# Where the load of the fifth expert buffer stands on SyncE: at the start of the program, or behind an operand move of pair 19

## The chip, the cores and the metric

The kernel runs on one core of one Trainium2 chip. The metric is the device time of one execution in microseconds (us); the time of a kernel is the median of its runs. TensorE (PE) multiplies matrices, VectorE (DVE), ScalarE (ACT) and GpSimd (POOL) work on tiles, and SyncE (SP) issues nearly all DMAs. Every engine works through its own instructions in a fixed order and waits for the others by semaphores.

## The reference

What is computed, cut to the core:

```python
# attention: q, k, v of 8 batches x 8 heads x 576 rows x 64
scores = (1 / sqrt(64)) * q @ k.T
scores = where(block(i) >= block(j), scores, -1e9)      # blocks of 64
attn = exp(scores - max) / (sum + 1e-9)
x = (attn @ v)  ->  4608 x 512
# soft mixture: 8 experts x 4 slots
logits = x @ phi                                       # 4608 x 32
d = softmax of logits over the rows;  c = over the slots
slot_out[e] = relu((d.T @ x)[e] @ w1[e]) @ w2[e]       # w1: 512 x 1024, w2: 1024 x 512
x = c @ slot_out
# bilinear layer
out = (((x @ W1) * (x @ W2)) @ W3) @ Wout
```

## The kernel before

**Attention** works on 32 pairs of heads, four for each batch. The loop `for n in range(N + 1)` in `Attn.run` walks through the string `ORDER` for each pair; it does the scores and exponentials of pair n (`Q..`, tile `sc`, lines 262 to 279), the row maxima of pair n + 2 (`M..`, tile `mx`, line 192), the products with `v` of pair n - 1, and the operands of pair n + 3 (`PH`, `PL`). To keep float32 accuracy each operand is a sum of two parts: `prep_hi` (ACT cast, line 151) makes the high part, `prep_lo` (GpSimd subtraction, line 159) the low part. They stand in the operand sets `set0` to `set3`, pair n in set n % 4. Of each pair, four DMAs from tile to tile (`move`, line 180, 288 KB each) put halves of these parts on other partitions: one by `PH`, three by `PL`. The last two of the three each overwrite what the one before read, so the three go one after another. `mx` of the pair needs all of them. The first three pairs are prepared by `prep_first` (lines 172 to 177), which has no moves; pair 3 is the first with moves.

The row maxima come in seven pieces, reduced by DVE (lines 196 and 202) into `bm`; `level2` (line 226, tile `l2`, with line 228 to `m`) takes the maximum of these with a mask, and `mra` (line 239, `mrow`) spreads it by TensorE; ACT's casts at lines 243 and 244 put it into the operand set. `acc` (line 295) is a sum of exponentials on GpSimd. In the trace the tiles `l2` and the operand sets have short names (`l`, `set`).

**Loads.** SyncE issues the query and key load of a pair (`raw`, 576 KB, line 137), `v` (line 144), the weights of the bilinear layer that are converted beside attention (`raw` from the weights, `raw64` in the order, line 654), two small `cs` moves for each batch (lines 428 and 429), and the expert weights, which `load_expert` reads (line 671). There are 16 of these, of 2048 KB each, for two matrices of eight experts, in a ring of five buffers; four buffers (`win0` to `win3`) lie where attention's tiles are and are loaded for the first time in its last four pairs. The fifth, `own`, lies by itself and is free from the start; its first load, i = 4, the first matrix of expert 2, is written in the program at `Q11` of n = 16, the middle of attention. Expert work reads it after attention, from 440 us on.

**Bilinear layer.** `wps` (line 730) forms the product of W3 and Wout beside the expert stage, from weights that DVE, ACT and GpSimd convert and split (lines 633 to 676). At the end `ab` (line 888) and its copy `abs` (ACT, line 891) and transposition `abT` (line 895) give two factors, copied into `own` (line 903, DVE and ACT). From these GpSimd forms `G16` (lines 927 to 929, tile `g_stage`) and DVE further products (lines 916 to 924). `Hp` (lines 938 and 944) multiplies with them; line 944 reads `G16`. Then a long row of matmuls (line 1042) makes the output.

**What sets the order.** The program isn't issued in the order in which it is written. A scheduler simulates a timeline and puts each instruction on its engine's queue when its inputs and its tile are free; the order on each engine is then fixed. `issue_after(x)` keeps what stands in it behind the instruction x. An instruction that is free early, such as the load of `own`, is put early.

Of the kernel before, what the change touches and what calls it, by code (L numbers as in the profile page):

```python
# [7 lines left out]
F32 = mybir.dt.float32  # L8
# [9 lines left out]
NB = 4  # L18
# [31 lines left out]
def warm(nc, keep, ps, n, w=128):  # L50

    for _ in range(n):
        nc.tensor.matmul(ps[:, 0:w], lhsT=keep["zeros"][:, 0:128], rhs=keep["zeros"][:, 0:w], start=True, stop=True)


class Attn:
# [120 lines left out]
        nc.gpsimd.tensor_tensor(R2[dn, 0:2 * S], raw[up], r1[up, 0:2 * S].bitcast(F32), op=ALU.subtract)  # L177

    def move(self, dst, src):
        self.nc.sync.dma_start(out=dst.bitcast(F32), in_=src.bitcast(F32))  # L180


    def max_tile(self, n, i):
# [349 lines left out]
    def run(self):  # L533
        nc, N = self.nc, self.n_pairs
        ML = self.ML
        LA = NB - 1
        self.load(0, 2)
        self.constants()
        for n in range(2, LA):
            self.load(n)  # L540
        warm(nc, self.keep, self.sc_p.tile([128, 1024], F32, tag="sc", name="warm"), WARM[0], 512)
        rows = []
        for n in range(ML):
            self.prep_first(n)
            if n == 0:
                self.constants2()
            for i in range(7):
                self.max_tile(n, i)
            self.level2(n)
            self.const_rows(n)  # L550
            row = self.mrow(n)
            rows.append(row)
            self.load_v(n)
        for m in range(ML, LA):
            if m < PF:
                with self.tc.issue_after(rows[0]):
                    self.prep_first(m)
            else:
                self.prep_hi(m)
                self.prep_lo(m)  # L560
        with self.tc.issue_after(row):
            for n in range(ML, NB):
                self.const_rows(n)
        self.load(LA)
        for n in range(N + 1):
            for t in (self.ORDER if n < N else self.LAST).split():
                k = int(t[1]) if t[1:].isdigit() else 0
                if t[0] == "M" and t != "MR":
                    self.max_tile(n + ML, k)
                elif t[0] == "Q":  # L570
                    self.qk_unit(n, int(t[1]), int(t[2]))
                    if t == "Q11" and self.after_scores:
                        if N - NB <= n < N:
                            self.after_scores(n - N + NB)
                        elif n == N // 2:
                            self.after_scores(NB)
                elif t[0] == "V":
                    self.pv(n - 1, k)
                elif t[0] == "A":
                    self.preadd(n, k)  # L580
                elif t == "PH":
                    self.prep_hi(n + LA)
                elif t == "PL":
                    self.prep_lo(n + LA)
                elif t == "L2":
                    self.level2(n + ML)
                elif t == "MR":
                    self.mrow(n + ML)
                elif t == "SU":
                    self.sums(n - 1)  # L590
                elif t == "LD":
                    self.load(n + LA + 1)
                    self.load_v(n + VL)
                elif t == "PT":
                    if n and n % NP_B == 0:
                        self.push_tail(n // NP_B - 1)
                elif t == "T":
                    self.step(1)
                elif t == "BG":
                    if self.background and n >= 1 and (n == 1 or n * 16 // BGP > (n - 1) * 16 // BGP):  # L600
                        with self.tc.issue_after(self.last_max[n + 1]) if n < BGF else nullcontext(), self.tc.issue_after(self.last_exp[n - 1]):
                            self.background.popleft()()
        while self.background:
            self.background.popleft()()
        self.step(100)
# [553 lines left out]
```

## Time and profile before

| | |
|---|---|
| median of 3 runs | 671.33 us (670.86 to 671.59) |
| profiled execution | 673.6 us |
| span of its instructions | 671.8 us |
| mean granted TensorE clock | 0.970 |
| busy: TensorE, DVE, POOL, ACT | 93%, 69%, 53%, 52% of the span |
| DMA | 141.45 MB, mean 211 GB/s |

The span runs from the first to the last instruction of the profiled execution; the time of that execution holds some 2 us around it. Roughly, attention fills the first 370 us and has its tail in the next 35, the expert stage with its weight loads lies beside that and reaches to about 515 us, and the bilinear layer the rest.

### The profile page before, as it was taken

How to read it: one execution, taken by the hardware profiler on the slowest of the kernel's cores; microseconds unless marked ns; L12 is line 12 of the kernel's file. 1: busy time of each engine (PE TensorE's matmuls, PEld its weight loads, DVE VectorE, ACT ScalarE, POOL GpSimd, SP SyncE). 2: the span in 40 equal slices, each digit the busy share in tenths (PEclk: the TensorE clock that was granted, in tenths of full speed). 3: DMA queues.
4: the chain of work that ended last, by engine and by line, in shares of the span. 5: the costliest groups of instructions: out<-in, count | busy, mean ns of one | idle time of the engine just before them, and what ended most of it. 6: DMA issues, size and time to landing. Idle time of an engine off the chain costs nothing. (4 is left out here: it accounts for less than half of the span.)

```text
span 671.8 us, 11777 instructions
## 1 busy us (share of the span) xinstructions
PE 622.7 (93%) x4423; PEld 454.3 (68%) x4423; DVE 460.2 (69%) x819; ACT 349.5 (52%) x645; POOL 354.0 (53%) x306
## 2 busy tenths in 40 slices
PE   4758989999999999999999998896999899999997
PEld 2646757777777777677777774533675487888886
DVE  8616766788859788577886466699863987555450
ACT  6653745656657575555656462244443425445541
POOL 8565785786768687766867471034323402122220
PEclk9987989999999999999999999797999999999999
DMA  9278687878788787778875859799991310755742
GB/s 315 71 189 222 163 217 185 200 194 221 211 213 219 199 223 173 212 198 217 219 180 129 286 190 349 292 381 401 398 385 59 112 54 25 252 184 183 255 155 94
DMA packets 53497, 141.45 MB, mean 211 GB/s; under 512 B 5928, under 2 KB 15656, under 8 KB 53416
## 3 DMA queue, kind: packets, MB, share of 16 engines
q1 hardware_dynamic: 53260, 140.63, 69.5%
q8 instruction: 35, 0.57, 0.4%
q14 instruction: 22, 0.18, 0.1%
q10 hardware_dynamic: 180, 0.07, 0.0%
HBM read 96.44 MB, written 10.32 MB: 159 GB/s over the span
## 5 line engine op out<-in xcount | busy, mean ns | idle before, releaser
L196 DVE TENSOR_REDUCE bm<-mx 128x8 f32<-128x512 f32 (+1 forms) x192 | 113.6, 618 | 44.8 <-PE mx L192 43.5
L262 PE MATMUL sc<-set 128*128 128x320 f32 (+4 forms) x704 | 132.6, 322 | 2.3 <-ACT set L244 1.3
L262 PEld LDWEIGHTS sc<-set 128*128 128x128 f32 x704 | 102.5, 197 | 12.6 <-issue 6.5
L192 PE MATMUL mx<-set 128*128 128x320 f32 (+4 forms) x384 | 87.9, 337 | 18.0 <-DMA set<-set 9.6
L295 POOL TENSOR_TENSOR acc<-PTa 128x640 f32<-128x640 f32 x31 | 49.8, 1606 | 83.1 <-PE sum L341 75.7
L192 PEld LDWEIGHTS mx<-set 128*128 128x128 f32 x384 | 67.2, 212 | 28.1 <-issue 9.7
L329 ACT COPY xT<-pv 128x320 f32<-128x320 f32 x64 | 25.6, 399 | 110.9 <-PE pv L327 97.9
L1042 PE MATMUL ops<-H,Ph 128*128 128x512 f32 x264 | 82.8, 395 | 0.0
L159 POOL TENSOR_TENSOR set<-raw,set 128x1152 fp32r<-128x1152 f32 x29 | 76.9, 2650 | 6.4 <-ACT set L151 6.4
L993 POOL TENSOR_TENSOR Pl<-rot,Ph 128x384 fp32r<-128x384 f32 x22 | 25.5, 1179 | 96.2 <-ACT Ph L991 96.2
L322 PE MATMUL pv<-PTa,v 128*64 128x320 f32 (+2 forms) x512 | 70.8, 376 | 0.0
L295 POOL TENSOR_TENSOR acc<-acc,PTb 128x640 f32<-128x640 f32 (+1 forms) x62 | 65.7, 1060 | 2.3
L271 ACT ACTIVATE PTa<-sc 128x960 f32<-128x960 f32 x64 | 59.3, 977 | 5.1 <-PE sc L262 5.1
L730 PE MATMUL wps<-wo,w 128*128 128x512 f32 x192 | 52.6, 417 | 6.8 <-ACT w L675 5.5
L1042 PEld LDWEIGHTS ops<-H,Ph 128*128 128x128 f32 x264 | 49.8, 189 | 11.9
L322 PEld LDWEIGHTS pv<-PTa,v 128*64 128x64 f32 x512 | 34.1, 138 | 28.8 <-issue 4.1
L1042 PE MATMUL ops<-H,Pl 128*128 128x512 f32 x132 | 52.2, 395 | 0.0
L730 PEld LDWEIGHTS wps<-wo,w 128*128 128x128 f32 x192 | 35.5, 194 | 22.7 <-ACT w L675 6.4
L1045 ACT COPY o<-ops 128x512 f32<-128x512 f32 x36 | 21.0, 587 | 56.6 <-PE ops L1044 56.4
L279 ACT ACTIVATE PTb<-sc 128x704 f32<-128x704 f32 x64 | 43.9, 693 | 8.7 <-PE sc L262 8.5
L322 PE MATMUL pv<-PTb,v 128*64 128x320 f32 (+1 forms) x256 | 43.5, 412 | 0.0
L676 POOL TENSOR_TENSOR w<-f,w 128x512 fp32r<-128x512 f32 x16 | 20.7, 1292 | 31.6 <-ACT w L675 31.1
(223 smaller groups left out, 1179.8 us busy)
## 6 DMA issues: line engine op xcount, KB each, us to landing
set<-set SPq DMA_DIRECT2D x116, 288.0 KB, 4.1
win<-in_moe_w SPq DMA_DIRECT2D x13, 2048.0 KB, 9.9
raw<-in_qk SPq DMA_DIRECT2D x31, 576.0 KB, 6.4
v<-in_v SPq DMA_DIRECT2D x32, 288.0 KB, 4.4
rot<-cs SPq DMA_DIRECT2D x44, 192.0 KB, 3.7
out<-o SPq DMA_DIRECT2D x11, 768.0 KB, 4.1
raw<-in_moe_w SPq DMA_DIRECT2D x16, 512.0 KB, 7.2
w3raw<-in_w3T SPq DMA_DIRECT2D x16, 512.0 KB, 11.0
```

Source lines behind the costliest of these rows:

```text
L159: nc.gpsimd.tensor_tensor(T1[:, 0:2 * S], self.raw.pop(n), flat(R1).bitcast(F32), op=ALU.subtract)
L192: nc.tensor.matmul(ps[:, o0:o0 + kn], lhsT=R1[:, h, q0:q0 + 128], rhs=T1[:, k0:k0 + kn], start=True, stop=True)
L196: self.last_max[n] = nc.vector.tensor_reduce(out, ps[:, 0:m].rearrange("p (n k) -> p n k", k=64), axis=AX.X, op=ALU.max).ins
L262: nc.tensor.matmul(ps[:, o0:o0 + qn * (qs.stop - qs.start)], lhsT=lt[:, k0:k0 + 128], rhs=rt[:, qs, q0:q0 + qn], start=st, stop=not st)
L271: nc.scalar.activation(out=PTa[:, h], in_=ps[:, 0:960], func=AF.Exp, scale=SCALE)
L279: self.last_exp[n] = nc.scalar.activation(out=PTb[:, S * h:S * h + w], in_=ps[:, 256:256 + w], func=AF.Exp, scale=SCALE).ins
L295: add = lambda o, a, b: eng.tensor_tensor(o, a, b, op=ALU.add)
L322: nc.tensor.matmul(ps[64 * h:64 * h + 64, q0 - lo:q1 - lo], lhsT=v[:, 128 * j + 64 * h:128 * j + 64 * h + 64], rhs=pt[:, h, o:o + q1 - q0] ...
L329: nc.scalar.copy(self.xTb[b % 2][:, p, lo:hi], ps[:, 0:hi - lo])
L730: nc.tensor.matmul(p, lhsT=a[:, o], rhs=b, start=c + i == 0, stop=c == 7 and i == 2)
L993: eng.tensor_tensor(Pl[:, k], p, Ph[:, k].bitcast(F32), op=ALU.subtract)
L1042: nc.tensor.matmul(ps, lhsT=a[:, k, r], rhs=b[:, k], start=n == 0, stop=False)
```

## The change

`move` keeps the last instruction that it issued. At `Q11` of n = 16 the load of `own` is put in `issue_after` with that instruction, the move that `PH` issued for pair 19. The load can't be put ahead of it any more.

```diff
     def move(self, dst, src):
-        self.nc.sync.dma_start(out=dst.bitcast(F32), in_=src.bitcast(F32))
+        self.last_move = self.nc.sync.dma_start(out=dst.bitcast(F32), in_=src.bitcast(F32)).ins
...
                         if N - NB <= n < N:
                             self.after_scores(n - N + NB)
                         elif n == N // 2:
-                            self.after_scores(NB)
+
+                            with self.tc.issue_after(self.last_move):
+                                self.after_scores(NB)
```

Lines behind the second place have numbers higher by two after the change. Since the load is no longer among SyncE's first DMAs, the scheduler orders other instructions anew, at three places.

**The start.** On DVE, in the first pairs, before (`set2_67` and `raw_142` are pair 2, `l2_199` and `m_201` the level-two maximum of pair 0, `bm1_120` and `l2_248` are pair 1):

```order
L228 TENSOR_REDUCE m_201<-l2_199 128x10
L196 TENSOR_REDUCE bm1_120<-mx_222 128x8
L196 TENSOR_REDUCE bm1_120<-mx_226 128x8
L196 TENSOR_REDUCE bm1_120<-mx_230 128x5
L196 TENSOR_REDUCE bm1_120<-mx_233 128x8
L196 TENSOR_REDUCE bm1_120<-mx_237 128x8
L196 TENSOR_REDUCE bm1_120<-mx_241 128x5
L202 TENSOR_REDUCE bm1_120<-mx_244 128x2x4
L172 CAST set2_67<-raw_142 64x1152
L174 CAST set2_67<-raw_142 64x1152
L226 TENSOR_TENSOR l2_248<-bm1_120,lmask_118 128x90
```

and on DVE at the same place after the change:

```order
L228 TENSOR_REDUCE m_201<-l2_199 128x10
L172 CAST set2_67<-raw_142 64x1152
L174 CAST set2_67<-raw_142 64x1152
L196 TENSOR_REDUCE bm1_120<-mx_222 128x8
L196 TENSOR_REDUCE bm1_120<-mx_226 128x8
L196 TENSOR_REDUCE bm1_120<-mx_230 128x5
L196 TENSOR_REDUCE bm1_120<-mx_233 128x8
L196 TENSOR_REDUCE bm1_120<-mx_237 128x8
L196 TENSOR_REDUCE bm1_120<-mx_241 128x5
L202 TENSOR_REDUCE bm1_120<-mx_244 128x2x4
L226 TENSOR_TENSOR l2_248<-bm1_120,lmask_118 128x90
```

The two casts of pair 2 moved from behind the seven reductions of pair 1 to ahead of them.

On GpSimd at the same place, before (`set3_68` and `raw_275` are pair 3, `raw_360` pair 4):

```order
L295 TENSOR_TENSOR acc_304<-PTa_277 128x2x320
L175 TENSOR_TENSOR set2_67<-raw_142,set2_67 64x1152
L295 TENSOR_TENSOR acc_304<-acc_304,PTa_277 128x2x192
L177 TENSOR_TENSOR set2_67<-raw_142,set2_67 64x1152
L295 TENSOR_TENSOR acc_304<-PTb_278,PTa_277 128x2x128
L159 TENSOR_TENSOR set3_68<-raw_275,set3_68 128x1152
```

and on GpSimd after:

```order
L175 TENSOR_TENSOR set2_67<-raw_142,set2_67 64x1152
L177 TENSOR_TENSOR set2_67<-raw_142,set2_67 64x1152
L295 TENSOR_TENSOR acc_304<-PTa_277 128x2x320
L159 TENSOR_TENSOR set3_68<-raw_275,set3_68 128x1152
L295 TENSOR_TENSOR acc_304<-PTb_278,PTa_277 128x2x128
L295 TENSOR_TENSOR acc_304<-acc_304,PTa_277 128x2x192
```

The operand work of pair 2 moved ahead of the first `acc`, and that of pair 3 behind the first `acc`.

**The middle.** On SyncE at pair 19 (`set3_68`; `set0_65` is pair 20, whose query and key load is `raw_2804`), before:

```order
L180 DMA set3_68<-set3_68 64x1152 x2
L137 DMA raw_2804<-in_qk 128x1152
L180 DMA set3_68<-set3_68 64x1152
L428 DMA cs_61<-cT_2460 4x32x128
L429 DMA cs_61<-cT_2460 32x64
L144 DMA v_2526<-in_v 128x576
L180 DMA set3_68<-set3_68 64x1152
L180 DMA set0_65<-set0_65 64x1152 x2
```

and on SyncE after:

```order
L180 DMA set3_68<-set3_68 64x1152
L673 DMA own_86<-in_moe_w1 128x4x1024
L180 DMA set3_68<-set3_68 64x1152
L137 DMA raw_2804<-in_qk 128x1152
L428 DMA cs_61<-cT_2460 4x32x128
L429 DMA cs_61<-cT_2460 32x64
L144 DMA v_2526<-in_v 128x576
L180 DMA set3_68<-set3_68 64x1152
L180 DMA set0_65<-set0_65 64x1152
L180 DMA set3_68<-set3_68 64x1152
```

The load stands between the first and the second of pair 19's four moves, and the last two of them moved behind other DMAs of the next batch.

**The end.** On TensorE at the hand-over to the bilinear layer, before (`w_5748` and `w_5786` are the last two converted pieces of W3):

```order
L895 MATMUL abT<-ident,abs 128x128 x4
L730 MATMUL wps<-wo,w_5748 128x512 x8
L730 MATMUL wps<-wo,w_5786 128x512 x12
L944 MATMUL Hp_5998<-W_5458,g_stage 32x512
L944 MATMUL Hp_5998<-W_5494,g_stage 32x512
L944 MATMUL Hp_5998<-W,g_stage 32x512 x5
L938 MATMUL Hp_5994<-g_stage_5874 128x512 x2
```

and on TensorE after:

```order
L897 MATMUL abT<-ident,abs 128x128 x4
L732 MATMUL wps<-wo,w_5748 128x512 x8
L946 MATMUL Hp_5998<-W_5458,g_stage 32x512
L946 MATMUL Hp_5998<-W_5494,g_stage 32x512
L946 MATMUL Hp_5998<-W,g_stage 32x512 x5
L732 MATMUL wps<-wo,w_5786 128x512 x2
L940 MATMUL Hp_5994<-g_stage_5874 128x512 x2
```

Seven matmuls of line 944 moved ahead of the last 12 of `wps`. On ACT at this place the copy `abs` moved two casts (line 991) forward; on DVE the last piece of the weight conversion moved backward.

## Rows read from the trace of the kernel before

**Rows 1.** Page, part 1: busy us (share of the span) and instructions.

```profile
PE 622.7 (93%) x4423; PEld 454.3 (68%) x4423; DVE 460.2 (69%) x819; ACT 349.5 (52%) x645; POOL 354.0 (53%) x306
```

**Rows 2.** Waits of TensorE: line, releaser, us in total, times, longest us.

```profile
PE mx L192 <- DMA set<-set: 9.6, 3, 5.7
PE mra L239 <- DVE m L228: 8.7, 4, 4.1
```

**Rows 3.** Timeline of SyncE's issues: start us, us of issuing, line, DMA.

```profile
7.11 0.43 SPq L671 DMA_DIRECT2D own<-in_moe_w x1
...
36.91 0.49 SPq L180 DMA_DIRECT2D set<-set  x1
```

**Rows 4.** DMA issues, 7.0 to 7.5 us: KB each, us to landing.

```profile
own<-in_moe_w SPq DMA_DIRECT2D x1, 2048.0 KB, 11.2
```

**Rows 5.** Timeline of DVE, start of attention: start us, us, line.

```profile
25.26 1.14 DVE L172 CAST set<-raw 64x1152 fp32r<-64x1152 f32 x1
...
27.11 2.65 DVE L226 TENSOR_TENSOR l<-bm,lmask 128x90 f32<-128x90 f32 x1
```

**Rows 6.** Timeline of GpSimd, start of attention; in brackets idle time, releaser.

```profile
24.23 1.55 POOL L295 TENSOR_TENSOR acc<-PTa 128x640 f32<-128x640 f32 x1 [7.36 <-DVE bm L196]
...
34.23 2.65 POOL L159 TENSOR_TENSOR set<-raw,set 128x1152 fp32r<-128x1152 f32 x1
...
39.12 2.62 POOL L159 TENSOR_TENSOR set<-raw,set 128x1152 fp32r<-128x1152 f32 x1
```

**Rows 7.** Timeline of TensorE, start of attention.

```profile
30.10 0.19 PE L239 MATMUL mra<-negI,m 128*2 128x64 f32 x1 [4.12 <-DVE m L228]
...
49.07 3.38 PE L192 MATMUL mx<-set 128*128 128x448 f32 x12 [5.66 <-DMA set<-set]
...
59.49 0.47 PE L192 MATMUL mx<-set 128*128 128x448 f32 x2 [2.21 <-ACT set L244]
59.80 0.94 PE L262 MATMUL sc<-set 128*128 128x256 f32 x6
```

**Rows 8.** Page, part 6: all moves and all `win` loads.

```profile
set<-set SPq DMA_DIRECT2D x116, 288.0 KB, 4.1
win<-in_moe_w SPq DMA_DIRECT2D x13, 2048.0 KB, 9.9
```

**Rows 9.** Timeline of ACT, start of attention.

```profile
35.85 1.81 ACT L271 ACTIVATE PTa<-sc 128x960 f32<-128x960 f32 x2
37.56 1.14 ACT L151 CAST set<-raw 128x1152 fp32r<-128x1152 f32 x1
```

**Rows 10.** DMA issues, 47.5 to 47.7 us.

```profile
set<-set SPq DMA_DIRECT2D x1, 288.0 KB, 7.8
```

**Rows 11.** Timeline of SyncE at pair 19.

```profile
219.03 1.93 SPq L180 DMA_DIRECT2D set<-set  x3
...
229.04 3.09 SPq L180 DMA_DIRECT2D set<-set  x3
```

**Rows 12.** DMA issues, 220.1 to 220.5 us.

```profile
set<-set SPq DMA_DIRECT2D x2, 288.0 KB, 5.0
```

**Rows 13.** Timeline of TensorE at pair 19.

```profile
234.73 0.81 PE L192 MATMUL mx<-set 128*128 128x448 f32 x3
```

**Rows 14.** Timeline of TensorE at pair 7.

```profile
93.95 0.47 PE L192 MATMUL mx<-set 128*128 128x448 f32 x2 [2.32 <-DMA set<-set]
```

**Rows 15.** Window: busy us of PE, PEld, DVE, ACT, POOL; clock; DMA share; GB/s.

```profile
90.00:100.00 10.00, 6.77 (x40) 5.45 (x37) 4.92 (x12) 4.66 (x7) 7.68 (x6) 0.83 0.91 231
```

**Rows 16.** Timeline of TensorE at the end of the expert stage.

```profile
526.51 0.66 PE L895 MATMUL abT<-ident,abs 128*128 128x128 f32 x4 [1.55 <-ACT abs L891]
526.93 5.24 PE L730 MATMUL wps<-wo,w 128*128 128x512 f32 x20
```

**Rows 17.** Timeline of DVE at the end of the expert stage.

```profile
528.14 0.89 DVE L903 COPY own<-abT 128x128 f32<-128x128 f32 x4
```

**Rows 18.** Timeline of GpSimd at the end of the expert stage.

```profile
531.38 0.79 POOL L929 TENSOR_TENSOR g_stage<-g_stage 128x128 f32<-128x128 f32 x1
```

## Prediction

> **What bounds the kernel now.** I read the views in this order: busy shares, the waits of TensorE, the timelines of the first 60 us, the granted clock by stage, and the landing times of DMAs. TensorE is busy 93% of the span [rows 1], so time comes only from stretches in which it stands still, or from a stand-still that is added. Its waits put the largest two at the start of attention: `mx`, the row-maximum matmul, waits 9.6 us in three places for the moves that fill an operand set, 5.7 us of it once, and `mra`, which spreads the maxima, waits 8.7 us for `m`, 4.1 us of it once [rows 2]. Both long ones lie before 50 us. After them the operands come just in time for a TensorE that hardly rests, so whatever the first pairs win or lose stays won or lost to the end.
>
> The load that is moved is SyncE's thirteenth DMA now, issued at 7.11 us and landing 11.2 us later [rows 3, 4], in a stretch in which TensorE waits for other things. That load itself is not what the start costs. What the order listing shows is that three places have another order after the change: the first five pairs, pair 19, and the hand-over to the bilinear layer. Each is a term of the sum.
>
> **The start (term A).** DVE and GpSimd now do the operand work of pair 2 (lines 172, 174 and 175) in front of the level-two maximum of pair 1 (line 226). The trace has line 172 at 25.26 us and line 226 at 27.11 us, and it takes 2.65 us there, beside a GpSimd operation of the other half [rows 5]. After the change the operand work stands behind `m` of pair 0, where DVE has idle time, and line 226 follows the seven reductions, which end at 25.2 us, where line 172 starts now. GpSimd's add `acc` runs from 24.23 to 25.78 us [rows 6]; letting line 226 wait for its end, and 0.6 us for it and line 228, gives `mra` at 26.4 instead of 30.10 us [rows 7]: 3.7 us. The 0.6 is what lies between the last two: 27.11 plus 2.65 is 29.76, `mra` 0.34 later, and 0.3 for a line 226 that nothing holds up. Without the wait for `acc` it would be 0.5 us earlier still, which is not counted. The row of line 226 [rows 5] is long where the two engines overlap; the Trainium skill, page "SBUF — State Buffer", section "Who interferes with whom", says that a DVE operation with two SBUF inputs and a GpSimd operation that reads SBUF exclude each other, the later one blocking fully. The 2.65 us agree with it; by it the 26.4 stands, without it 25.9.
>
> `mra` is not the end of it, for the next waits are `mx` of pairs 3 and 4. Pair 3's low part (line 159) is on GpSimd at 34.23 us for 2.65 us, behind the operand work of pair 2 and two `acc` adds [rows 6]. Afterwards it is the second operation behind the operand work, at 26.0 us, done at 28.7. Its first move leaves SyncE at 36.91 us now [rows 3], so at 28.7 then. Three moves follow one another, each waiting for the one before. With 4.1 us for each, the median of 116 moves [rows 8], the last lands at 41.0 us, against `mx` at 49.07 us [rows 7], 8.1 us sooner.
>
> Pair 4 then decides. Its ACT cast (line 151) is at 37.56 us, behind the two exponentials of 35.85 us [rows 9]; after the change it stands between those two. From `mra` to the first exponential are 5.75 us now (30.10 to 35.85), so that one begins at 26.4 plus 5.75 or 32.15 us, takes half of 1.81 us, and the cast ends 1.14 us later, at 34.2. Line 159 of that pair follows on GpSimd, which two adds may still hold for a moment, and ends at 36.9 to 37.5 us instead of 41.74 (39.12 plus 2.62) [rows 6]; I take 37.2. Now its chain of three moves lasts from there to `mx` at 59.49 us [rows 7], with 7.8 us for the second move [rows 10]. With 4.1 us for each the last lands at 49.5 us; with 7.8 for the second, as now, at 53.2. I take 51, nearer to the median because fewer loads are between them there, hence a gain of 8.5 us; nine matmuls that are now behind this `mx` are done ahead of it, 1.4 us more at 0.94 us for six [rows 7]. **A is minus 10.0** (9.9), and 7.7 and 12 are its ends: 53.2 us on one side, 49.5 and a lower clock less on the other. From pair 5 on every step comes with the same shift, TensorE's too, so the 10 us persist.
>
> **The middle (term B).** The load now stands on SyncE between the first move of pair 19 (`PH`) and its three other ones. In the trace the first of those three is the last of the three issued from 219.03 us on, and the last of them is the first of the three at 229.04 us [rows 11]. Queued behind the load are also the query and key load of pair 20, two `cs` moves and a `v` load. A load of 2048 KB lands in 9.9 us by the median of thirteen, a move at this place in 5.0 us [rows 8, 12]. If the move directly behind the load lands when it does, it is 4.9 us late, and the two moves that wait for it as well. The cover is small: the last move lands at 229.04 plus 4.1 or 233.1 us, and `mx` of pair 19 begins at 234.73 us [rows 13], so 1.6 us are covered and TensorE stands still for 3.3. A stand-still costs more than itself here: the one of 2.32 us at pair 7 stands in a stretch of 10 us with 0.83 of the full clock [rows 14, 15], 1.7 us in 10. I add that 1.7. **B is plus 5.0.** Its ends are 0, if the move doesn't wait for the load's packets, and 9, if the delay is the 11.2 us of this very load at the start [rows 4] and the loads queued between the moves add theirs: a stand-still of 5.6 us and two stretches of lower clock, 3.4 us.
>
> Here the trace decides little by itself, since it has no move directly behind a 2 MB load. By the Trainium skill, page "DMA: Bandwidth & Descriptors", section "Queues, rings and completion order", each DMA engine takes the descriptors of one issuing queue in ring order, which speaks against this change: the moves wait for the whole load. By that rule B is the 5.0; if moves could overtake, B would be 0.
>
> **The end (term C).** TensorE stands still for 1.55 us before `abT` at 526.51 us, then does 20 `wps` matmuls in 5.24 us, to 532.2 us [rows 16]. They hide the chain that makes `G16`: DVE's copies of `abT` at 528.14 us, ACT's copies, and three GpSimd operations, of which the last is at 531.38 us for 0.79 us [rows 17, 18]. `G16` is ready at 532.17, just in time for line 944. After the change the seven matmuls of line 944 stand ahead of the last 12 `wps`. The copy `abs` stands two casts earlier on ACT, so `abT` comes about 1.5 us sooner, but TensorE then has only eight `wps` (2.1 us) and reaches line 944 at about 527.6 us. DVE's copies are ahead of less work of the weight conversion, but still behind the products of line 990, and I get them at 527.1 to 528.1 us: `G16` at 531.2 to 532.2. So TensorE stands still for 4 us instead of 1.55, and 12 `wps` (3.1 us) are still to be done when it goes on: plus 2.2 to 3.1 us, of which I take 2.6. The stand-still of 4 us calls for a lower clock by the same row as above, 1.7 us [rows 14, 15]. **C is plus 4.3**, its ends 1.8 (no lower clock, earliest copies) and 5.5.
>
> The added line itself, and one DMA issue more or less at a place, cost nothing: SyncE is idle between moves. The rest of the differences in order, in the final stage, move one matmul and one output DMA and are counted as zero.
>
> **The sum.** Minus 10.0 plus 5.0 plus 4.3 is minus 0.7 us. The profiled execution took 673.6 us, its span 671.8, the median of the runs is 671.33 us; I take the difference against the median, for the profiled execution is 2.3 us above it. That gives 670.6 us. A measurement can tell about 0.2% from no change, 1.3 us, so faster means below 670.0 and slower above 672.7.
>
> **The rivals.**
> - *The queue in the middle is longer.* For it: behind the load are four other DMAs, and the second move of pair 19 queues behind pair 20's 576 KB. Against it: a median of 9.9 us already holds some queueing [rows 8]. B is then 9 and the time 674.6, slower. It decides when the stand-still at pair 19 exceeds 5.3 us: B is then above 7.0, and the sum above plus 1.3.
> - *The load is hidden.* If the moves behind it land in their usual 4 to 5 us, TensorE sees nothing at 234.73 us: 665.6. Against it: the raw loads behind the load at the start are not used until later, so nothing there shows an overtaking.
> - *The start gives back less.* If pair 4's second move takes 7.8 us as now, `mx` starts at 53.2 us, A is 7.7, and the time is 672.9.
> - *The end costs nothing.* If DVE's copies come 3 us earlier, because conversion work moved behind them, `G16` is ready when TensorE arrives: 666.3. Against it: the products of line 990 and the casts stand in front of them in either order.
> - *The change does not do what it says* is out: the order listing shows the load at its new place.
>
> **How the numbers follow.** The forecast of 670.6, own range 667.5 to 673.5, has a chance of 0.50; the longer queue 0.18; the hidden load 0.12; the weaker start 0.12; the free end 0.08. Each of A, B and C is larger than their sum, and both signs hold much. From the forecast 0.21 lies below 670.0, 0.18 within and 0.11 above; with the hidden load and the free end faster has 0.41, with about half of the weaker start same has 0.24, and slower 0.35. For 8 in 10 I take 665.4 to 675.0, which leaves out the outer parts of the hidden load and of the longer queue.
>
> **What would show it.** Right, if `mra` of pair 1 is at about 26.4 us and `mx` of pairs 3 and 4 at about 41 and 51; if the first move behind the load lands some 10 us after its issue and TensorE waits about 3.3 us for the moves at pair 19; if line 946 (944 before) waits about 4 us for GpSimd. Wrong, if `mx` of pair 4 still starts after 53 us, if pair 19 shows no wait or one above 5.3 us, if a later pair has a new wait, or if the waits come out as said and the clock does not fall after them (3.4 us less).

## The result and the profile after

The changed kernel takes 675.57 us, the kernel before 671.15 us by its 20 runs (671.33 by the three that the prediction had); the ratio is 1.0069, with a 95% interval of 1.0042 to 1.0095. It is slower by 0.7%, 4.4 us. One of the changed kernel's 20 runs, at 843.9 us with a mean granted clock of 0.659, is left out of the ratio. The forecast was 670.6, the range ended at 675.0. The profiled execution of the changed kernel took 674.65 us, its span is 672.8 us.

All three places of the prediction show in its profile. Waits of TensorE, with the columns of [rows 2]:

```profile
PE mx L192 <- DMA set<-set: 14.2, 5, 6.2
...
PE mra L239 <- DVE m L228: 5.4, 3, 3.3
PE Hp L946 <- POOL g_stage L931: 4.3, 1, 4.3
```

The wait for `m` has lost 3.3 us, the wait for moves has grown by 4.6 us and has a new longest one of 6.2, and `Hp` waits for `G16`, which it did not. The timeline of TensorE puts them in place; the first three lines answer to [rows 7], the fourth to [rows 13], the last three to [rows 16]:

```profile
26.27 0.19 PE L239 MATMUL mra<-negI,m 128*2 128x64 f32 x1 [1.25 <-DVE m L228]
...
39.67 1.71 PE L192 MATMUL mx<-set 128*128 128x448 f32 x6 [1.95 <-DMA set<-set]
...
51.48 0.69 PE L192 MATMUL mx<-set 128*128 128x448 f32 x3 [1.72 <-DMA set<-set]
...
233.10 1.19 PE L192 MATMUL mx<-set 128*128 128x448 f32 x3 [6.19 <-DMA set<-set]
...
521.04 0.66 PE L897 MATMUL abT<-ident,abs 128*128 128x128 f32 x4
521.45 2.10 PE L732 MATMUL wps<-wo,w 128*128 128x512 f32 x8
527.85 3.57 PE L946 MATMUL Hp<-W,g_stage 128*32 128x512 f32 x14 [4.30 <-POOL g_stage L931]
```

`mra` of pair 1 is 3.8 us earlier, `mx` of pair 3 9.4 us and of pair 4 8.0 us. Pair 19 then stands still for 6.2 us, and line 946 for 4.3 us. The landing of the move behind the load, as in [rows 12], and the granted clock behind both stand-stills (columns of [rows 15]):

```profile
set<-set SPq DMA_DIRECT2D x1, 288.0 KB, 13.5
```

```profile
225.00:240.00 15.00, 8.81 (x64) 7.31 (x61) 5.36 (x12) 6.26 (x10) 6.84 (x6) 0.77 0.89 234
```

```profile
527.00:537.00 10.00, 9.15 (x39) 5.22 (x40) 9.90 (x17) 2.56 (x5) 2.55 (x2) 0.83 0.08 22
```

To follow a shift through the program I took the start of `mra` of each pair, of the first `ab` matmul and of the last output matmul from TensorE's timeline. Five columns say where the time goes in the kernels below; the last column is the measured ratio to the kernel before with its interval. Each row is one profiled execution; before_again (the second row) and half_size were run only once, so they have no ratio.

| kernel | `mra` of pair 14 | pair 18 to 19 | pair 22 to 23 | pair 24 to `ab` | `ab` to last output | ratio |
|---|---|---|---|---|---|---|
| before | 187.8 | 12.2 | 15.5 | 212.2 | 147.6 | 1 |
| before, again | 186.5 | 12.2 | 12.2 | 210.2 | 148.4 | |
| changed | 178.3 | 20.6 | 12.2 | 210.9 | 152.7 | 1.0069 (1.0042 to 1.0095) |
| split | 181.5 | 12.2 | 17.7 | 212.3 | 152.7 | 1.0033 (1.0005 to 1.0062) |
| behind | 178.7 | 18.7 | 12.2 | 211.7 | 152.7 | 1.0026 (0.9993 to 1.0059) |
| half_size | 177.2 | 15.7 | 16.7 | 210.3 | 152.5 | |
| act_queue | 179.2 | 15.6 | 12.2 | 211.4 | 152.7 | 1.0027 (0.9996 to 1.0058) |
| end_fence | 177.7 | 20.0 | 12.2 | 213.8 | 156.6 | 1.0127 (1.0086 to 1.0167) |
| conv_first | 178.8 | 18.9 | 12.3 | 211.1 | 152.5 | 1.0061 (1.0032 to 1.0091) |
| conv_ahead | 179.4 | 21.3 | 12.2 | 214.0 | 148.8 | 1.0042 (1.0012 to 1.0072) |
| parts_conv | 179.5 | 13.5 | 15.8 | 211.8 | 152.6 | 1.0014 (0.9981 to 1.0047) |
| start_before | 187.4 | 20.6 | 12.2 | 213.0 | 148.2 | 1.0099 (1.0064 to 1.0134) |
| early | 182.9 | 12.2 | 12.2 | 212.9 | 147.6 | 0.9914 (0.9889 to 0.9940) |
| early_conv | 178.7 | 12.2 | 12.4 | 212.6 | 147.6 | 0.9924 (0.9900 to 0.9948) |

### The profile page after: what moved, and what is told of

Its sections match the earlier page's. It is cut to its first block, busy times and chain, and to the rows that moved or that the text cites. A ratio compares the mean times of both kernels' runs of the same rounds, so it can differ in the third digit from the quotient of the medians.

```text
span 672.8 us, 11771 instructions
## 1 busy us (share of the span) xinstructions
PE 618.5 (92%) x4423; PEld 450.0 (67%) x4423; DVE 460.3 (68%) x819; ACT 349.7 (52%) x645; POOL 355.5 (53%) x306
## 3 DMA queue, kind: packets, MB, share of 16 engines
q1 hardware_dynamic: 53260, 140.63, 69.7%
## 5 line engine op out<-in xcount | busy, mean ns | idle before, releaser
L262 PEld LDWEIGHTS sc<-set 128*128 128x128 f32 x704 | 103.5, 199 | 13.5 <-issue 4.8
L192 PE MATMUL mx<-set 128*128 128x320 f32 (+4 forms) x384 | 85.1, 326 | 20.7 <-DMA set<-set 14.2
L192 PEld LDWEIGHTS mx<-set 128*128 128x128 f32 x384 | 64.2, 201 | 30.9 <-issue 14.9
L159 POOL TENSOR_TENSOR set<-raw,set 128x1152 fp32r<-128x1152 f32 x29 | 77.0, 2654 | 11.3 <-ACT set L151 11.2
L995 POOL TENSOR_TENSOR Pl<-rot,Ph 128x384 fp32r<-128x384 f32 x22 | 27.6, 1273 | 96.1 <-ACT Ph L993 96.1
```

The source lines that it names most:

```text
L159: nc.gpsimd.tensor_tensor(T1[:, 0:2 * S], self.raw.pop(n), flat(R1).bitcast(F32), op=ALU.subtract)
L192: nc.tensor.matmul(ps[:, o0:o0 + kn], lhsT=R1[:, h, q0:q0 + 128], rhs=T1[:, k0:k0 + kn], start=True, stop=True)
L262: nc.tensor.matmul(ps[:, o0:o0 + qn * (qs.stop - qs.start)], lhsT=lt[:, k0:k0 + 128], rhs=rt[:, qs, q0:q0 + qn], start=st, stop=not st)
L995: eng.tensor_tensor(Pl[:, k], p, Ph[:, k].bitcast(F32), op=ALU.subtract)
```

## The experiments

My theory after this: the start gives some 8 us by the order of DVE and GpSimd, the load in SyncE's queue takes 8 us at pair 19, and the new order at the hand-over takes 4 to 5 us. The rivals stand in each expectation. Of each edit only the lines that matter are shown.

**before_again.** Expected: 

> The kernel before, unchanged, with a profile of another execution. If the wait of 1.67 us for pair 22's moves and the lower clock behind it belong to that one execution, this profile has no lower clock between 280 and 290 us and a span some 3 us shorter, or the same thing at another pair. If they belong to the order, they stand at the same place again, mx of that pair at 282.35 us.

The wait did not come back. (It is that of pair 23 in the count of this document; the expectation calls it 22.) In the kernel before the wait is this line of TensorE's timeline:

```profile
282.35 0.70 PE L192 MATMUL mx<-set 128*128 128x448 f32 x3 [1.67 <-DMA set<-set]
```

The same stretch of the two executions, columns of [rows 15], in the kernel before:

```profile
280.00:290.00 10.00, 8.33 (x56) 6.74 (x50) 5.01 (x11) 6.14 (x10) 7.82 (x6) 0.83 0.80 208
```

and in its second profile:

```profile
280.00:290.00 10.00, 10.00 (x80) 7.38 (x76) 8.10 (x15) 6.49 (x11) 8.79 (x7) 1.00 0.80 206
```

So 3.3 us of the first profile belong to one execution. A difference between two traces is read stage by stage, and 1 to 3 us at pairs 7, 15 and 23 are no evidence by themselves.

**split.** The load in four pieces, each behind the last move of a pair:

```diff
-                        elif n == N // 2:
-                            with self.tc.issue_after(self.last_move):
-                                self.after_scores(NB)
...
                 elif t == "PL":
                     self.prep_lo(n + LA)
+                    if 0 <= n - N // 2 < 4:
+                        with self.tc.issue_after(self.last_move):
+                            self.after_scores(NB, n - N // 2)
```

Expected: 

> The change, but the 2 MB load is cut into four of 512 KB, each behind the last move of one pair (19 to 22); every other engine has the order of the changed kernel. Theory (the moves of pair 19 wait for the whole load in SyncE's queue, 6.2 us and a lower clock, 8.4 in all): the wait of mx at pair 19 goes, no pair has more than 2 us in its place, and the time is 7 to 9 us below the changed kernel, 0.993 to 0.996 of the kernel before. Rival (the wait comes from where pair 19's moves stand among the other DMAs, or from 2 MB more of traffic in this stretch): waits of 2 us and more stay in this stretch, and the time is that of the changed kernel, 1.003 to 1.010.

Half of each. Pair 19 takes 12.2 us, as in the kernel before: the 8.4 us there are gone, with DVE, GpSimd, ACT and TensorE in the order of the changed kernel. But the time falls only to 1.0033, and a wait comes at pair 23, whose moves have the fourth piece ahead of them:

```profile
278.42 0.70 PE L192 MATMUL mx<-set 128*128 128x448 f32 x3 [3.90 <-DMA set<-set]
```

Pair 23 closes a batch like pair 19 and has the two `cs` moves in its queue. The pair takes 5.5 us more than 12.2; since one of the two executions of the kernel before lost 3.3 us there without any piece, how much of it the piece costs isn't shown.

**behind.** The whole load behind the last move of pair 19:

```diff
                 elif t == "PL":
                     self.prep_lo(n + LA)
+                    if n == N // 2:
+                        with self.tc.issue_after(self.last_move):
+                            self.after_scores(NB)
```

Expected: 

> The change, but the whole load stands behind the last move of pair 19, so that the first two moves of pair 20 stand directly behind it; the other engines have the order of the changed kernel. Theory (whichever move stands behind the load waits for all of it): the wait at pair 19 goes and one of 4 to 6 us for moves comes at pair 20; the time is within 2 us of the changed kernel, 1.004 to 1.010 of before. Rival (pair 19 is a special place, with two cs moves and a v load in its queue): no wait over 2 us at pair 20, time 0.993 to 0.997.

The loss stayed in size (6.5 us instead of 8.4), but the wait was another than I expected. Not pair 20's move decided, but a weight load for the conversion that stands behind the load: ACT waits for it (first line of the next two views), `lg` waits for ACT (second).

```profile
238.77 0.67 ACT L638 ACTIVATE m<-raw 128x512 bf16<-128x512 f32 x1 [8.64 <-DMA raw<-in_moe_w]
```

```profile
239.78 2.19 PE L383 MATMUL lg<-xT,phib 128*64 128x288 f32 x8 [4.92 <-ACT Lg L385]
```

Whatever stands behind the load waits, not the moves alone. Pair 20's moves were late too. Here the trace has the landing of the load, issued at 221.29 us, and of the second move behind it, issued at 222.91 us:

```profile
own<-in_moe_w SPq DMA_DIRECT2D x1, 2048.0 KB, 10.4
```

```profile
set<-set SPq DMA_DIRECT2D x1, 288.0 KB, 12.2
```

So the load landed at 231.7 us and this move 3.5 us later.

**half_size.** The first half of the load at the place of the change, the second behind the last move of pair 21:

```diff
                             with self.tc.issue_after(self.last_move):
-                                self.after_scores(NB)
+                                self.after_scores(NB, 0)
...
+                    if n == N // 2 + 2:
+                        with self.tc.issue_after(self.last_move):
+                            self.after_scores(NB, 1)
```

Expected: 

> The change, but only the first 1 MB of the load stands at its place behind the first move of pair 19; the second 1 MB stands behind the last move of pair 21. All engines but SyncE have the order of the changed kernel. Theory (the moves wait for the bytes ahead of them in the queue): the move behind the load lands 8.5 to 10 us after its issue instead of 13.5, and mx of pair 19 waits 1.5 to 3 us instead of 6.2. Rival (a fixed price of the place, whatever the size): the wait stays at 5 us or more.

In this one execution it came as the theory had it, but for 0.2 us: SyncE's timeline shows the move behind the load and, as the second line, the one that waits for its landing: 10.2 us, where 8.5 to 10 were expected, against 13.6 in the changed kernel (213.04 and 226.62).

```profile
208.75 1.19 SPq L180 DMA_DIRECT2D set<-set  x1
...
218.94 0.46 SPq L180 DMA_DIRECT2D set<-set  x1
```

The load itself, of 1 MB, was issued at 207.89 us and landed at 216.9 us, 2.0 us ahead of the move:

```profile
own<-in_moe_w SPq DMA_DIRECT2D x1, 1024.0 KB, 9.0
```

`mx` of pair 19 waits 1.9 us (the profile names ACT's line 243 as the releaser, but the last move landed at 226.14 us and `mx` starts at 226.23), and the pair takes 15.7 us, 3.5 more than before. The second half costs 4.6 us at pair 23.

**act_queue.** ACT issues the load, which is tied to ACT's cast of pair 19 in place of the move:

```diff
-        self.nc.sync.dma_start(out=v, in_=...)
+        (self.nc.scalar if i == NB else self.nc.sync).dma_start(out=v, in_=...)
```

Expected: 

> The change, but ACT issues the 2 MB load, behind its cast of pair 19, instead of SyncE; the bytes and the moment are about the same, and SyncE's moves have a queue without it. Theory (the price is the order within SyncE's queue): the moves of pair 19 land in 4 to 8 us, mx waits under 2.5 us there, and the time is 4 to 8 us below the changed kernel, 0.995 to 1.002 of before. Rival (2 MB more of traffic in this stretch slows every move, whatever the queue): the moves land 10 us and more after their issue and mx waits 4 us or more.

The wait is that of the theory, the landing that of the rival. The wait falls to 1.75 us and the pair to 15.6 us, 5.0 of the 8.4 us less. But the moves still land late, the two issued between 211.5 and 212.5 us (the last of pair 18, whose landing alone is recorded, and the first of pair 19) and pair 19's second at 214.0 us:

```profile
set<-set SPq DMA_DIRECT2D x2, 288.0 KB, 8.3
```

```profile
set<-set SPq DMA_DIRECT2D x1, 288.0 KB, 11.4
```

That is 8 to 11 us instead of 4 to 5: 2 MB more in this stretch delay a move of another queue as well. How much of the 5.0 us is the order within one queue isn't shown, since the moment wasn't the same: the load left at 208.24 us, 5.8 us before pair 19's second move, where in the changed kernel it left 0.8 us before it (212.22 and 213.04).

**end_fence.** Line 946 behind the last `wps`:

```diff
             def h_last(f):
                 g = f % 4
-                nc.tensor.matmul(Hp[4][32 * g:32 * g + 32], ...)
+                with tc.issue_after(self.last_wps):
+                    nc.tensor.matmul(Hp[4][32 * g:32 * g + 32], ...)
```

Expected: 

> The change, but line 946 may only stand behind the last wps matmul on TensorE. Start and middle are those of the changed kernel. Theory (4.3 us of wait for G16 and a lower clock behind it make the loss of 4.4 to 5 us at the end): no wait for G16, and the time is 4 to 5 us below the changed kernel, 0.999 to 1.002 of before. Rival (the conversion of the last piece of W3, which also moved, holds TensorE instead): TensorE waits for w at wps instead, over 2 us, and the time falls by less than 2 us.

The rival. The wait for `G16` is gone and TensorE waits for the last piece of W3 instead, over 6 us of the 11.6 in this line (the other 5.5 stand in the kernel before too); and the ratio is the highest of all:

```profile
PE wps L732 <- ACT w L677: 11.6, 2, 6.2
```

**conv_first.** The copies of `abT` behind the last conversion:

```diff
+                        with tc.issue_after(self.last_f if m == 0 else self.last_hi):
-                        eng(dst[:, 4 * h:4 * h + 4, ...], v[:, :, m, h])
+                            eng(dst[:, 4 * h:4 * h + 4, ...], v[:, :, m, h])
```

Expected: 

> The change, but DVE's and ACT's copies of abT may only stand behind the conversion of the last piece of W3 (as in the kernel before); TensorE's order listing then has abT, 20 wps and line 946 again. Start and middle are those of the changed kernel. Theory (the loss of 4 to 5 us at the end comes from the conversion having moved behind the copies, which leaves TensorE only 8 wps to do while G16 is made): no wait over 1 us for G16, the wait of 1.5 us for abs may come back, and from the first ab matmul to the last output matmul it takes what it takes in the kernel before, 147.6 us, instead of 152.7; time 0.999 to 1.002 of before. Rival (the wait for G16 is due to GpSimd and stays whatever TensorE has to do): 151 to 153 us there, 1.005 to 1.009.

Neither came as written, though the stretch and the time lie in the rival's range. There is no wait for `G16`, but the same time, 4.3 us in two waits, is spent in waiting for the converted weights (3.6 us for ACT, 0.7 for GpSimd), and the stretch takes 152.5 us, nearly what it took without this remedy:

```profile
524.89 0.73 PE L732 MATMUL wps<-wo,w 128*128 128x512 f32 x2 [3.63 <-ACT w L677]
```

So putting back TensorE's order and the place of the copies doesn't take the loss away.

**conv_ahead.** The last two conversions in front of `soT`:

```diff
-                nc.vector.tensor_copy(dst..., p[:, 0:128])
+                with tc.issue_after(self.u_ops[-1]) if name == "soT" else nullcontext():
+                    nc.vector.tensor_copy(dst..., p[:, 0:128])
...
-            nc.scalar.copy(sos, so)
+            with tc.issue_after(self.m_ops[-2]):
+                nc.scalar.copy(sos, so)
```

Expected: 

> The change, but the copy soT may only stand behind the first step of the last conversion on DVE, and ACT's copy sos only behind the last but one squaring of a conversion, as both do in the kernel before. Start and middle are those of the changed kernel; TensorE has 20 wps ahead of line 946 again. Theory (in the changed kernel two conversion steps stand behind soT on DVE, which waits 11.7 us for sumT, so that the last two pieces of W3 come late; that, not TensorE's order, is the loss at the end): neither a wait of over 1 us for G16 nor one for w at wps; from the first ab matmul to the last output matmul 147.5 to 149 us instead of 152.7; time 0.998 to 1.002 of before. Rival (the loss is there as soon as the end starts with a lower clock or other traffic, whatever DVE's order): 151 us and more, 1.004 to 1.009.

In the changed kernel DVE stands idle in front of `soT` while a conversion is queued behind it:

```profile
515.80 0.29 DVE L784 COPY soT<-sumT 128x128 f32<-128x128 f32 x1 [11.71 <-PE sumT L782]
```

That gap alone is not the difference: in the kernel before DVE stands idle there too, 7.8 us for ACT and 1.7 in front of `soT`. What differs is what comes behind: the last step of the last conversion (line 641, 643 after) starts 6.6 us after the first `ab` in the kernel before (7.4 in its second profile), 12.1 us in the changed kernel and 6.8 us in conv_ahead.

With the conversions ahead, from the first `ab` on 148.8 us are needed, as the theory says, 3.9 less, and neither `G16` nor `w` is waited for over 1 us there. But `sos` and `soT` now come later, and 2.3 us of new waits stand ahead of `ab`:

```profile
518.05 1.08 PE L782 MATMUL sumT<-sel,sos 128*128 128x32 f32 x8 [0.92 <-ACT sos L881]
...
520.81 1.07 PE L892 MATMUL ab<-wA,soT 128*32 128x512 f32 x2 [1.37 <-DVE soT L785]
```

From pair 24 to the last output it is 362.8 us against 363.6 in the changed kernel and 358.6 to 359.8 in the kernel before. By the time the loss shrinks from 1.0069 to 1.0042, with intervals that overlap. The place of the conversion on DVE carries the wait for `G16`; that this alone is the loss isn't shown.

**parts_conv.** Pieces behind the moves of pairs 19, 20, 21 and 23, together with conv_first:

```diff
+                    if n - N // 2 in (0, 1, 2, 4):
+                        with self.tc.issue_after(self.last_move):
+                            self.after_scores(NB, min(n - N // 2, 3))
```

Expected: 

> Two remedies together: the load in four pieces of 512 KB, each behind the last move of a pair (19, 20, 21 and 23, so that none stands ahead of the moves of pair 23), and the copies of abT behind the last conversion as in conv_first. Theory (the start gives 8 to 10 us, the middle and the end took them): 661 to 665 us, 0.985 to 0.992 of before, with no wait over 2 us for moves between 200 and 300 us. Rival (the gain of the start is given back at the later pairs 7, 15 and 23 anyway, since their moves come just in time): 0.994 to 1.000.

The expectation failed: 1.0014, no change that can be told. No wait for moves above 2.0 us is left between 200 and 300 us, but three waits of 1.1 to 2.0 us remain: of `lg` for ACT at pair 19, of `mx` at pair 22, for which the profile names no releaser, and of `mx` for moves at pair 23. These pairs take 1.4, 3.5 and 3.6 us longer, 8.5 together (pair 23 without a piece ahead of its moves, as in one execution of the kernel before), and the end is as slow as in conv_first.

**early.** The load at the start, behind the query and key loads of pairs 2 and 3:

```diff
         self.load(LA)
+        with self.tc.issue_after(self.last_load):
+            self.after_scores(NB)
```

Expected: 

> The load of own stands at the start again, but behind the query and key loads of pairs 2 and 3 instead of ahead of them; DVE and GpSimd have the order of the changed kernel in the first pairs, and TensorE has line 946 behind all wps, as before. Theory (the 10 us at the start are the order of DVE and GpSimd, not the 2 MB, which land while the queue is idle): mra of pair 1 at 26 to 27 us, mx of pair 4 at 50 to 53 us, no wait at pair 19 beyond 2 us; time 0.984 to 0.992 of before. Rival (the 2 MB in the first 20 us are themselves the loss): mx of pair 4 at 55 us or later and the time 0.996 to 1.002.

665.98 us, 0.9914 of the kernel before: the lowest ratio of all. The load is issued at 17.62 us (SyncE's timeline), and `mra` of pair 1 comes as in the changed kernel (TensorE's):

```profile
17.62 0.43 SPq L671 DMA_DIRECT2D own<-in_moe_w  x1
24.79 0.56 SPq L180 DMA_DIRECT2D set<-set  x1
```

```profile
26.49 0.19 PE L239 MATMUL mra<-negI,m 128*2 128x64 f32 x1 [1.91 <-DVE m L228]
...
53.54 1.89 PE L192 MATMUL mx<-set 128*128 128x448 f32 x6 [5.05 <-DMA set<-set]
```

The next move comes 7 us after it, so the load has that stretch nearly to itself (343 GB/s from 18 to 25 us). `mx` of pair 4 is at 53.5 us, half a microsecond beyond what the theory allowed and 2.1 us later than in the changed kernel, but pair 19 takes 12.2 us and the end 147.6. The start isn't quite that of the changed kernel: ACT's cast of pair 4 stands behind both exponentials, so that GpSimd's line 159 of that pair starts at 35.77 us instead of 34.09. `mra` of pair 4 is at 64.4 us (63.2 in early_conv), where the changed start gives 59.7 to 62.7, and the gain in time, 5.8 us, is less than the 8 of the start.

**early_conv.** early and conv_ahead together. Expected: 

> As early, with the two conversion orders of conv_ahead besides. Theory (each of the two remedies takes away its own loss, and the end of early has nothing left to gain): within 0.3% of early. Rival (the end of early still loses by the conversion behind soT): 2 to 5 us below early.

0.9924, within the interval of early: at this end the second remedy has nothing to give.

**start_before.** The start of the kernel before, the rest changed:

```diff
-                with self.tc.issue_after(rows[0]):
+                with self.tc.issue_after(rows[0]), self.tc.issue_after(self.last_max[1]):
                     self.prep_first(m)
```

Expected: 

> The change, but the operand work of pair 2 may only stand behind pair 1's row maxima on DVE, as in the kernel before. The load keeps its place at pair 19; TensorE's order at the end comes out as before (20 wps ahead of line 946). Theory (the 8 to 10 us of the start come from the place of pair 2's operand work; the load at pair 19 costs 8 us): mra of pair 1 at 29 us or later instead of 26.3, mx of pair 4 between 52 and 59 us instead of 51, the wait at pair 19 again 4 to 6 us, so some 0 to 8 us from the start, 8 of loss in the middle and none at the end: 1.000 to 1.014 of before. Rival (the start is faster because the 2 MB are out of its way, whatever DVE's order): mra of pair 1 at 26 to 27 us, mx of pair 4 at 51 us, and the time 0.996 to 1.001.

The theory. With no 2 MB at the start, but with the two casts of pair 2 in front of line 226 again, `mra` of pair 1 and `mx` of pair 4 are back near where they were in [rows 7], and pair 19 waits as in the changed kernel:

```profile
29.81 0.21 PE L239 MATMUL mra<-negI,m 128*2 128x64 f32 x1 [3.31 <-DVE m L228]
...
58.10 1.19 PE L192 MATMUL mx<-set 128*128 128x448 f32 x3 [4.20 <-DMA set<-set]
...
242.07 1.19 PE L192 MATMUL mx<-set 128*128 128x448 f32 x3 [5.93 <-DMA set<-set]
```

It takes 1.0099. `mra` of pair 4 is at 69.7 us, 70.0 in the mean of the two profiles of before: with the old order the start is as slow without the 2 MB as with them. So the gain of the start is order, not bytes; early agrees, with the 2 MB at the start and `mra` of pair 1 at 26.5 us.

## Why the prediction was wrong

**Right: which three places, and the sign of each.** No fourth place shows that differs beyond what the two profiles of the kernel before differ by.

**Right in kind, 1.8 us too large: the start.** Predicted were `mra` at 26.4, `mx` of pair 3 at 41 and of pair 4 at 51 us; the trace has 26.27, 39.67 and 51.48. `mra` of pair 14 is at 178.9 us in the mean of the nine kernels with the changed start and the load not at the start, 187.1 in the mean of the two profiles of before: 8.2 us, where term A said 10.0. At pair 4 the same means are 60.6 and 70.0, 9.4 us. Most of what A took too much is in its last step, that everything after pair 4 keeps its distance: pair 7, whose moves have little slack, gives 1.1 us back (17.5 us from `mra` of pair 6 to that of pair 7, 16.4 in the kernel before).

**Wrong: the size of the middle.** This is the step that failed. The kind was right (the move behind the load, 1.6 us of cover, a lower clock after it), and so was the pair. Term B let the move behind the load land with the load, 9.9 us after its issue by [rows 8]; it landed after 13.5 us (12.5 to 13.5 in the five kernels with the load at this place), the wait was 6.2 us instead of 3.3, and the stretch lost 8.4 us instead of 5.0.

Two things in that step were wrong. The 9.9 us are not the median of thirteen loads: the trace of the kernel before has the landing of only three `win` loads, after 7.6, 9.9 and 20.2 us. And the moves behind a load landed after it, not with it: the second of them 3.5 us after it in behind, the first 2.0 us in half_size (by the issue of the move that waits for it). The landing of the load itself isn't recorded in the changed kernel, so how the 3.6 us divide between the two stays open.

The traffic has a part as well, though no run shows its size alone. Nine of the thirteen `win` loads run when SyncE has nothing but weights to load, at 381 to 401 GB/s (page, part 2, 437 to 504 us). Around pair 19 the same engines carried 261 GB/s from 212 to 226 us (the view of DMA traffic, changed kernel; kernel before, 7.5 to 18.3 us, behind it):

```profile
DMA packets 1005, 3.65 MB, mean 261 GB/s; under 512 B 93, under 2 KB 156, under 8 KB 1002
```

```profile
DMA packets 1169, 3.92 MB, mean 363 GB/s; under 512 B 93, under 2 KB 93, under 8 KB 1169
```

By these rates 2 MB take 8.0 us around pair 19 and 5.8 us at the start, an estimate. The DMA share of 0.74 to 0.96 from 210 to 240 us in the profile before said that there was little room; I read the landing time and not the share.

**The end: right in size, its cause only in part.** The wait for `G16` is 4.3 us where 4 was said, a lower clock follows (0.83), and from `ab` to the last output it takes 152.7 instead of 147.6 to 148.4 us, 4.3 to 5.1, where term C said 4.3. What I called the cause, TensorE's order, is only where it shows: with that order undone (end_fence, conv_first) the wait turns up at the weights. What goes with the loss is the place of the last conversion on DVE. Over the fourteen profiles its last step starts 6.5 to 7.4 us after the first `ab` where the stretch takes 147.6 to 148.8 us, and 9.6 to 12.1 us after it where it takes 152.5 to 156.6. In start_before the load stands at pair 19 and the stretch takes 148.2 us, so the load's place is not the reason by itself. Whether the conversion is all of the loss stays open, since conv_ahead in its profile lost ahead of `ab` most of what it won behind it.

**The sum.** Minus 8.2 plus 8.4 plus 4.3 to 5.1 is 4.5 to 5.3, against 4.4 measured. The rival *the queue in the middle is longer* (B of 9, 674.6 us) is what came in size, and its point of decision, a wait above 5.3 us, was met. Of its two reasons one came: the first move took 13.5 us, more than the 11.2 it reckoned with, but the loads queued between the moves added nothing (pair 19's last two moves left 3.3 us apart, 3.8 in the kernel before). A and B missed in the same direction, so nothing evened out. The range missed it by 0.6 us because its upper end joined that rival to the full gain of the start; a somewhat smaller A beside a B near its end was left out, though both were named.

**The rule on rings.** The move behind the load waited for it: 13.5 us behind 2 MB, 10.2 behind 1 MB. The Trainium skill, page "DMA: Bandwidth & Descriptors", section "Queues, rings and completion order", says that an issuer's descriptors are taken in ring order on each DMA engine; these runs agree, though they don't separate that order from the traffic. The same section says that an engine takes turns between the queues for which it has work; act_queue agrees, with 8 to 11 us for a move that shares its engines with the load of another queue.

## What to carry to other kernels

A load that can wait is not free in the middle of a stretch with a DMA share of 0.8 and moves that come just in time: price it by the bytes queued around it at the rate of that stretch (here 3.65 MB in 14 us), not by its landing time elsewhere, look how many landings a median rests on, and name what stands behind it in its queue, other loads too. Look for the stretch in which the queue is idle (here 18 to 25 us) before cutting the load in pieces; in pieces, kernels still lost 5.5 us at pair 23 (split) and 8.5 us at three pairs (parts_conv), a part of it perhaps without the pieces. And where a scheduler sets the order, one moved DMA can change the compute engines' order at far places: compare the orders first, since the gain of the start here came from order and not from the bytes, and the loss at the end went with an order too.

## What the runs showed of the hardware

The same 2 MB on ACT's queue still made moves on SyncE's queue take 8 to 11 us instead of 4 to 5: a queue of its own did not shield them from the traffic. Behind a load in one queue the first move landed 2.0 us after the load (half_size), the second 3.5 us (behind). And waits of TensorE that differ little had a different sequel: 1.67 us ahead of 282.35 us in the kernel before stand in 10 us (280 to 290) with a mean granted clock of 0.83, while 1.55 us ahead of 526.51 us (the same execution) stand in a stretch of full clock, 1.00 over 520 to 560 us.
